# Sparse attention and Fourier mixing on one core: the block sums' share of the values in 64x32 tiles for batches 2 and 3, and batch 0's second weight tile converted behind the copies of the transposed tiles

## The chip, the core and the metric

The kernel runs on one core of one Trainium2 chip. TensorE (PE) multiplies matrices, VectorE (DVE) and ScalarE (ACT) work on elements, GpSimd (POOL) is used a little, and SyncE (SP) issues most DMAs. The metric is the device time of one execution in microseconds (us), as the median of several runs; less is better.

## The reference

The kernel computes attention over a window and over block summaries, then a Fourier mixing with a two-layer network. Cut to what matters:

```python
# q, k, v: (4, 8, 768, 64); block 32, window 16
k_sum = k.reshape(B, H, nb, block, D).max(axis=3)
v_sum = v.reshape(B, H, nb, block, D).mean(axis=3)
scores_l = scale * q @ k.T                      # kept where |i - j| < window
scores_s = scale * q @ k_sum.T + np.log(block)
a = softmax(concatenate([masked scores_l, scores_s]))
x = a @ concatenate([v, v_sum])                 # then (4, 768, 512), heads side by side
mixed = real(fft(fft(x, axis=1), axis=2))
u = x + mixed
un = (u - mean(u)) / sqrt(var(u) + 1e-6)        # over the last axis
out = u + maximum(un @ w_ch1, 0) @ w_ch2        # w_ch1: 512 x 2048, w_ch2: 2048 x 512, float64
```

The two weights come as float64. The kernel converts them to float32 on chip, from their two 32-bit words.

## The kernel before, in words

The four batches run one after another. Each goes through attention (four pairs of heads), the Fourier mixing, a hidden layer and an output layer. TensorE works on one batch's hidden and output layers while the attention of the next batch is fitted in between. Batch 0's attention stands first, in an order written out by hand. After that the order of the instructions on each engine is set at compile time by a planner that takes the ready instruction which the program emits earliest; `high_priority(600)` moves what it wraps ahead, and `issue_after(mark)` puts what it wraps behind the marked instruction of the same engine. DMAs of the first part that go through `fetch` (L549) stay in program order on SP's queue.

**Values of batches 1 to 3** (`values`, L821). One call handles a pair of heads. `av[0]` and `av[1]` are two banks of PSUM. L829 adds the near tokens' share with 48 matmuls: 64 rows of the contraction, 32 output rows, 65 columns; four places of output rows and two halves of the contraction make eight tiles of the array. L834 then adds the block sums' share: for three `t` and two halves `r` one matmul each, with 64 contraction rows, 128 output rows and 130 columns. A reciprocal (L839) and a product (L842) finish the pair's part of `x`. Ahead of it come `scores` (L785), whose exponentials are multiplied by the 0/1 mask `near` (for batch 1's first two pairs not at L802 but at L1051), `sum_scores` (L805), which needs the key maxima `km` (L700), and `scale_sums` (L814).

**Hidden and output layers** (`gen_hidden` L1358, `gen_out` L1414). A product of 2x2 blocks is made with seven products, in three accumulators X, Y and Z. Seven weight blocks per tile are needed: four converted ones and three sums of them (`_left_sums` L477), and seven blocks of the activations `u` (`_right_sums` L483). Hidden tile j starts with the blocks A11 and A12 of its weight tile; only its second use of X and its use of Z need the sums of `u`, and its copies of X and Z are made by ACT (L1388 to L1396), its additions by DVE.

**Weights of batch 0** (`convert` L1099, `make` L1121, `plan` L1072). `words` holds four pieces of raw weight words; a weight tile has two. `exponents` (L1092) takes the exponent bits on DVE (L1096) and rescales them on ACT (L1097); `convert` then takes the mantissa (L1109 on DVE, L1110 on ACT), combines sign and exponent (L1112), adds the low word (L1114) and multiplies (L1116). `make` adds the sums, and stores the tile to DRAM for the later batches. `load_raw` (L1078), called at the start of each conversion, fetches pieces for the tile after it. `plan` lists the tiles in order as (layer, tile, stage): a tile is begun once its stage is in `issued`, and if there is a mark of the stage's name its instructions are put behind that mark.

**Batch 0 between mixing and hidden layer** (`gen_fourier` L1224). After the mixing (L1297, L1299), DVE forms mean and variance and normalises (L1279, mark `mx`), PE transposes the six normalised tiles (L1349), and ACT or DVE copies each to `u` (L1350); the last copy is on DVE and its mark is `u`. Then come the sums of `u`. At L1558 to L1565 `drive` interleaves this with the weights and with the attention of batch 1, which are both written as generators: a step of a generator ends at each `yield`. Of the four attention steps at L1564, the second emits `scores(1, 1)` and `values(1, 0)`, the third `sum_scores(1, 1)` and `load_values(1, 2)`, the fourth the product with `near` for pair (1, 1) and `prepare(1, 2)`, which transposes that pair's queries and keys and takes its key maxima on DVE.

## Time and profile before

| what | us |
|---|---|
| three runs | 792.73, 796.05, 793.62 |
| their median | 793.62 |
| the profiled execution | 790.53 |
| its span, first to last instruction | 788.6 |

The profile shows one execution. PE records are matmuls (PE) and weight loads (PEld); the end of a matmul record is modelled, so the start of the next one is the firmer number. The granted TensorE clock was 0.999 over the span. Groups of the profile that the change touches (count of records, busy time in all, mean of one):

| line, engine, what | records | busy us | mean ns |
|---|---|---|---|
| L829 PE, near share of the values | 1152 | 15.8 | 225 |
| L834 PE, block sums' share of the values | 144 | 12.5 | 291 |
| L1349 PE, transposes of the normalised tiles, batch 0 | 48 | 6.5 | 279 |

Each float32 matmul of the program appears as two records. Of L834's 144 records 96 belong to batches 2 and 3. A timeline line gives start, time, engine, line, operation, out<-in, shapes and count; in brackets stands the idle time before it and what ended it.

### The profile page before, as it was taken

Reading aid. Unit: us, or ns where it says so; the run is one execution under the profiler, and the core shown is the slowest. Engines: PE = TensorE matmul, PEld = TensorE weight load, DVE = VectorE, ACT = ScalarE, POOL = GpSimd, SP = SyncE. Lnnn points to the kernel's source line nnn. Section 1 sums busy time; section 2 is a strip of 40 time slices with the busy share of each in tenths; the row PEclk is TensorE's granted clock in tenths of the full one; section 3 lists DMA queues with packets and bytes.
Section 4 is the critical chain, followed back from the end, with each engine's and each line's share of the span. In section 5 each row is a group of like instructions: output and inputs, shape, how many; then the busy total and the mean of one; then the engine's idle time right before and its main releaser. Section 6 shows DMA issues by size and latency. Waiting matters only on the chain.

```text
span 788.6 us, 14351 instructions
## 1 busy us (share of the span) xinstructions
PE 776.1 (98%) x5920; PEld 562.9 (71%) x5920; DVE 491.2 (62%) x1017; ACT 224.1 (28%) x491; POOL 49.2 (6%) x87
## 2 busy tenths in 40 slices
PE   9999999999999999999999999999999999999997
PEld 6778455445588866787578866788569865886686
DVE  5899978697889566652759545552667623533352
ACT  3565656236536022100236012200136012001200
POOL 0000000000000030200310020300220000000000
PEclk9999999999999999999999999999999999999999
DMA  9999887796855279965442169611513163106001
GB/s 214 184 266 237 206 275 196 242 260 221 232 161 155 49 231 261 204 103 177 154 144 87 54 209 212 184 55 31 223 44 134 54 220 134 47 0 234 0 28 57
DMA packets 133353, 121.82 MB, mean 154 GB/s; under 512 B 94464, under 2 KB 114912, under 8 KB 133088
## 3 DMA queue, kind: packets, MB, share of 16 engines
q1 hardware_dynamic: 132160, 118.53, 53.9%
q0 software_dynamic: 576, 2.10, 0.8%
q8 instruction: 48, 0.79, 0.4%
q10 hardware_dynamic: 544, 0.20, 0.1%
q14 instruction: 25, 0.20, 0.1%
HBM read 97.22 MB, written 23.59 MB: 153 GB/s over the span
## 4 chain that ended last, share of the span: by engine, by line
PE 87%; DVE 9%; ACT 1%; issue 1%; DMA 1%; POOL 0%; SPq 0%; DVEq 0%; POOLq 0%
PE hx L1377 19%; PE ox L1446 18%; PE hz L1377 10%; PE oz L1446 9%; PE hy L1377 5%; PE oy L1446 5%; PE o L1423 4%; PE y L1258 3%; PE sc L793 2%; PE mx L1217 2%; PE av L829 1%; PE av L834 1%; PE qk L718 1%; DVE x L571 1%; PE unt L1349 1%
## 5 line engine op out<-in xcount | busy, mean ns | idle before, releaser
L1377 PE MATMUL hx<-u,w 128*128 128x384 f32 x512 | 185.4, 491 | 1.5 <-ACT h L1394 0.7
L1377 PEld LDWEIGHTS hx<-u,w 128*128 128x128 f32 x512 | 94.9, 190 | 70.3 <-ACT p L800 3.8
L1377 PE MATMUL hz<-u,w 128*128 128x384 f32 x256 | 93.7, 487 | 0.2 <-DVE u L571 0.2
L1446 PE MATMUL oz<-w,s 128*128 128x256 f32 x336 | 81.3, 380 | 0.0
L1446 PE MATMUL ox<-w,s 128*128 128x256 f32 x336 | 80.1, 380 | 0.0
L1446 PE MATMUL ox<-w,h 128*128 128x256 f32 x336 | 79.6, 381 | 0.0
L571 DVE TENSOR_TENSOR x<-ox,x 128x256 f32<-128x256 f32 x84 | 35.5, 423 | 66.2 <-PE ox L1446 65.9
L1377 PEld LDWEIGHTS hz<-u,w 128*128 128x128 f32 x256 | 48.4, 190 | 34.1 <-DVE u L571 0.8
L1446 PEld LDWEIGHTS ox<-w,h 128*128 128x128 f32 x336 | 63.1, 190 | 10.8 <-issue 1.2
L1446 PEld LDWEIGHTS oz<-w,s 128*128 128x128 f32 x336 | 63.3, 190 | 8.9 <-DVE x L571 0.4
L1446 PEld LDWEIGHTS ox<-w,s 128*128 128x128 f32 x336 | 63.2, 190 | 9.0 <-DVE x L571 0.3
L1388 ACT COPY h<-hx 128x384 f32<-128x384 f32 x32 | 15.3, 479 | 187.1 <-PE hx L1377 187.1
L571 DVE TENSOR_TENSOR h<-hy,h 128x384 f32<-128x384 f32 x32 | 17.8, 557 | 48.4 <-PE hy L1377 48.2
L1377 PE MATMUL hy<-u,w 128*128 128x384 f32 x128 | 46.8, 487 | 0.6 <-DVE h L571 0.6
L571 DVE TENSOR_TENSOR h<-hx,h 128x384 f32<-128x384 f32 x32 | 17.8, 556 | 44.1 <-PE hx L1377 43.9
L1423 PE MATMUL o<-w,h 128*128 128x512 f32 x96 | 42.3, 595 | 0.7 <-DVE w L571 0.7
L1407 ACT ACTIVATE h<-hx 128x384 f32<-128x384 f32 x32 | 15.7, 490 | 88.3 <-PE hx L1377 88.2
L1446 PE MATMUL oy<-w,h 128*128 128x256 f32 x168 | 40.1, 380 | 0.0
L571 DVE TENSOR_TENSOR x<-oz,x 128x256 f32<-128x256 f32 x42 | 17.8, 424 | 30.4 <-PE oz L1446 30.1
L1377 PEld LDWEIGHTS hy<-u,w 128*128 128x128 f32 x128 | 24.1, 190 | 16.9 <-DVE h L571 0.7
L1446 PEld LDWEIGHTS oy<-w,h 128*128 128x128 f32 x168 | 31.8, 190 | 4.4
L1423 PEld LDWEIGHTS o<-w,h 128*128 128x128 f32 x96 | 18.0, 190 | 22.7 <-issue 20.7
(167 smaller groups left out, 1072.8 us busy)
## 6 DMA issues: line engine op xcount, KB each, us to landing
w<-dw SPq DMA_DIRECT2D x44, 896.0 KB, 5.7
words<-in_moe_w_ch_dram SPq DMA_DIRECT2D x32, 512.0 KB, 5.7
dw<-w SPq DMA_DIRECT2D x12, 896.0 KB, 7.5
vw<-in_v_dram SPq DMA_DIRECT2D x47, 192.0 KB, 6.1
out_dram<-x SPq DMA_DIRECT2D x23, 256.0 KB, 2.0
vb<-in_v_dram SPq DMA_DIRECT2D x24, 192.0 KB, 6.8
kn<-in_k_dram SPq DMA_DIRECT2D x9, 384.0 KB, 6.1
qn<-in_q_dram SPq DMA_DIRECT2D x9, 384.0 KB, 7.6
```

The lines of the kernel that those rows point to most:

```text
L571: return nc.vector.tensor_tensor(out=out, in0=in0, in1=in1, op=op).ins
L718: nc.tensor.matmul(ps[D * e:D * (e + 1), s:S2:HT], src[:, e, h, s, :], ident, start=True, stop=True)
L793: ins = nc.tensor.matmul(ps[h][r:r + 64, i, :], kt[rows, o:o + 64], qt[rows, o:o + BLOCK], start=True, stop=True)
L829: nc.tensor.matmul(av[r][32 * j:32 * (j + 1), t, :], p[rows, h, i - NB2 * h, :], vw[rows, i, :], start=(t == 0), stop=False, skip_group_ch ...
L834: ins = nc.tensor.matmul(av[r][:, t:t + HT + 1:HT, :], pm[rows, P * t:P * (t + 1)], vs[rows], start=False, stop=(t == HT - 1), skip_group_ ...
L1217: nc.tensor.matmul(out, y[:, g], table, start=False, stop=True, skip_group_check=True)
L1258: nc.tensor.matmul(y, fgs[b][par][:, st, P * g:P * (g + 1)], fs[par][:, g % 2, st, :], start=(st == 0), stop=(st == n - 1))
L1377: ins = nc.tensor.matmul(ps, w[:, a, kk, :], u[:, r, kk, :], start=start and kk == 0, stop=stop and kk == 1, skip_group_check=True)
L1388: nc.scalar.copy(out=c11, in_=X)
L1407: nc.scalar.activation(out=c21, in_=X, func=AF.Relu)
L1423: nc.tensor.matmul(ps, h[:, n, hf, P * t:P * (t + 1)], wt[2, b, j][:, 2 * hf:2 * hf + 2, :], start=(n, hf) == (0, 0), stop=(n, hf) == (NC ...
L1446: nc.tensor.matmul(ps, left[a][:, n, :], wt[2, b, j][:, r, :], start=start and n == 0, stop=stop and n == NC - 1, skip_group_check=True)
```

## The change

In `values` the loop over the output rows is split for batches 2 and 3: instead of one matmul with 128 output rows there are four with 32 rows each, at the four places that L829 uses. Batch 1 keeps 128. In `plan`, weight tile (1, 1) moves from stage `mx` to a new stage `u`, the last copy of the transposed tiles. The product with `near` for pair (1, 1), and those instructions of `prepare(1, 2)` that run on DVE, move behind a new mark `w`, the last of the sums of weight tile (1, 1). The steps at L1564 are emitted in another order: three steps of the attention with the mixing, then fifteen steps of the weights, then the fourth attention step. A helper now remembers the last instruction of `tt`.

```diff
+    final = [None]
+
     def tt(out, in0, in1, op):
-        return nc.vector.tensor_tensor(out=out, in0=in0, in1=in1, op=op).ins
+        final[0] = nc.vector.tensor_tensor(out=out, in0=in0, in1=in1, op=op).ins
+        return final[0]
...
         for t in range(HT):
-            for r in range(2):
-                rows = slice(64 * r, 64 * (r + 1))
-                ins = nc.tensor.matmul(av[r][:, t:t + HT + 1:HT, :], pm[rows, P * t:P * (t + 1)], vs[rows],
-                                       start=False, stop=(t == HT - 1), skip_group_check=True)
+            n = 32 if b > 1 else P
+            for o in range(0, P, n):
+                for r in range(2):
+                    rows = slice(64 * r, 64 * (r + 1))
+                    ins = nc.tensor.matmul(av[r][o:o + n, t:t + HT + 1:HT, :], pm[rows, P * t + o:P * t + o + n], vs[rows],
+                                           start=False, stop=(t == HT - 1), skip_group_check=True)
...
-                    with tc.issue_after(marks["u"]) if g else ExitStack():
+                    with tc.issue_after(marks["w", 1]) if g else ExitStack():
                         (tt if g else gtt)(held[0][:, h], held[0][:, h], near[:, h], ALU.mult)
             if n1 and n1 != (1, 1):
-                prepare(*n1, *((1,) if b > 1 else ()))
+                with tc.issue_after(marks["w", 1]) if n1 == (1, 2) else ExitStack():
+                    prepare(*n1, *((1,) if b > 1 else ()))
...
-    plan = [(1, 0, ("fold", 0)), (1, 1, ("mx", 0)), (1, 2, ("mx", 0)), (2, 0, ("mx", 0)), (1, 3, ("h", 0, 0)), (2, 1, ("mx", 0)),
+    plan = [(1, 0, ("fold", 0)), (1, 1, ("u", 0)), (1, 2, ("mx", 0)), (2, 0, ("mx", 0)), (1, 3, ("h", 0, 0)), (2, 1, ("mx", 0)),
...
             _left_sums(tt, wv)
+            marks["w", j] = final[0]
...
-            if t == NST - 1:
-                marks["u"] = ins.ins
+            if b == 0 and t == NST - 1:
+                marks["u", 0] = ins.ins
+                issued.add(("u", 0))
...
-    drive((mixing, 6, 600), (first(weights, 15), 15, 0), (first(attn, 4), 4, 0))
+    drive((first(attn, 3), 3, 0), (mixing, 6, 600))
+    for _ in first(weights, 15):
+        pass
+    next(attn)
     block_sums(1, 1)
```

## The prediction

> **What bounds the kernel now.** I read the page first: the engine row, then the chain of work that ended last.

> ```profile
> PE 776.1 (98%) x5920; PEld 562.9 (71%) x5920; DVE 491.2 (62%) x1017; ACT 224.1 (28%) x491; POOL 49.2 (6%) x87
> ...
> PE 87%; DVE 9%; ACT 1%; issue 1%; DMA 1%; POOL 0%; SPq 0%; DVEq 0%; POOLq 0%
> ```

> TensorE (PE) is the bound nearly everywhere. The chain's 9% on VectorE (DVE) lies in batch 0 ahead of the first hidden product; for 48 to 105 us DVE is busy almost without a break (windows: 8.00 of 8.00 us in 77 to 85, 7.00 of 7.00 in 90 to 97). So the two parts of the change are priced separately: a PE saving in batches 2 and 3, which reaches the end whole, and a DVE reordering in batch 0.

> Second view, the timeline of PE around one values call of batch 2 (start, time, line, x count of records):

> ```profile
> 309.66 1.20 PE L829 MATMUL av<-vw,p 64*32 64x65 f32 x96
> 310.79 0.94 PE L834 MATMUL av<-vs,p 64*128 64x130 f32 x12
> 311.66 1.24 PE L1377 MATMUL hx<-u,w 128*128 128x384 f32 x3
> ```

> A float32 matmul shows as two records, so L834's 12 are six matmuls. Starts tell more than times: L834's block holds PE for 311.66 - 310.79 = 0.87 us; in the raw starts L829's last record stands 0.145 us before L834's first weight load, and L834's last 0.200 us before the next stage's. All unsplit calls of the two batches show these three numbers.

> Third view, PE's timeline as batch 0 goes from its transposes (unt) to its first hidden products:

> ```profile
> 77.11 1.53 PE L1349 MATMUL unt<-ident,big 128*128 128x128 f32 x12
> 79.46 1.10 PE L811 MATMUL ss<-qt,km 64*32 64x384 f32 x8 [0.82 <-DVE km L700]
> ...
> 85.64 0.91 PE L1377 MATMUL hz<-u,w 128*128 128x384 f32 x2 [0.22 <-DVE u L571]
> 86.94 1.53 PE L1377 MATMUL hx<-u,w 128*128 128x384 f32 x4 [0.38 <-DVE u L571]
> ...
> 95.55 0.91 PE L1377 MATMUL hy<-u,w 128*128 128x384 f32 x2 [0.56 <-DVE h L571]
> ```

> Three things are waited for: the key maxima (km), the sums of u, and a hidden add (h). DVE's timeline says why:

> ```profile
> 77.16 0.69 DVE L1096 TENSOR_SCALAR words<-words 128x1024 int32<-128x1024 int32 x1
> 77.77 0.69 DVE L1109 TENSOR_SCALAR w<-words 128x1024 int32<-128x1024 int32 x1
> 78.37 0.95 DVE L700 TENSOR_REDUCE km<-kt 128x24 f32<-128x768 f32 x1
> 79.23 1.22 DVE L1112 SCALAR_TENSOR_TENSOR words<-words 128x1024 int32<-128x1024 int32 x1
> 80.36 1.23 DVE L1114 SCALAR_TENSOR_TENSOR w<-words,w 128x1024 f32<-128x1024 uint32 x1
> 81.50 1.29 DVE L1350 COPY u<-unt 128x512 f32<-128x512 f32 x2
> 82.70 1.22 DVE L571 TENSOR_TENSOR w<-w,words 128x1024 f32<-128x1024 f32 x1
> 83.83 1.76 DVE L571 TENSOR_TENSOR u<-u 128x1536 f32<-128x1536 f32 x1
> ```

> The conversion of weight tile (1, 1) stands ahead of km, of the copies of the last transposed tiles and of the sums, though hidden tile 0 needs only weight tile (1, 0).

> [...] Here the first 32 records of L829 start 7 ns apart, each group of eight tiles 57 ns after the last. [...] from the 33rd L829 slows to 11.2 ns a record (64 in 716 ns)[...]

> **Part A, the values.** In eight calls (two batches, four pairs) 12 records of L834 become 48, of 32 output rows each, in L829's own mode. Removed: the switch between the two. The cost now, from L829's last start to the next stage's weight load: 0.145 + 0.870 = 1.015 us. After: each of eight tiles gets six records. The moving operand still has 130 columns, and L834's rounds now start 0.112 us apart. First record about 0.06 after L829's last, five steps of 0.112, eight starts of 7 ns (0.05), exit 0.200: 0.87 us, saving 0.145 a call. Bounds: if the first record follows at once (0.017), 0.83 (saving 0.19). [...] If L829's slow pace came from eight moving streams[...], 48 records of twice the columns take 48 x 22.4 ns = 1.08, with 0.200 1.28: a loss of 0.26. Against that last stand the first 32 records, at full pace with the same eight streams. Taken: 8 x 0.145 = **-1.2 us**; ends -1.5 and +2.1. The 288 added record pairs cost nothing[...]; they need one per 0.112/8 = 14 ns. [...]

> **Part B, weight tile (1, 1).** Its instructions on DVE: L1096 0.60, L1109 0.60, L1112 1.13, L1114 1.14, product 1.13, sums 0.33 + 0.60 + 0.33 = 5.9 us; on ACT L1097 1.06 and L1110 0.95. All now follow the copies. PE's excess in the third view, by starts: km 78.37 to 79.46, 1.09 against 0.20 at the earlier unt-to-ss hand-over, 0.89; sums 0.70 and 0.87 against a step of 0.32, 0.38 and 0.55; the add 0.83 against 0.20, 0.63. Together 2.45 us.

> What becomes of each: DVE is free at 77.25, km is done at 78.1, before unt ends: 0.89 gone. The copies run at 78.8 to 79.4, the sums 79.4 to 82.9 instead of 83.8 to 88.2: PE does not wait for them. **Next late is ACT**: the second use of X (hx at 86.94) also needs ACT's copy of X, at 85.72 behind 8.8 us of continuous ACT work from 76.97, which the change shuffles but does not shorten. So hx starts at about 86.2, 0.74 sooner, and with the other half of Z's product (0.65) already done. I take 1.4 us at the end of hidden tile 0, 91.6 instead of 93.0.

> What is added: the near product of pair (1, 1) (two of 0.47) and the key maxima of pair (1, 2) (0.86) wait for tile (1, 1)'s last sum; behind the near product stands values (1, 1), 2.2 us of PE. Tile (1, 1) is ready at 79.4 + 3.5 (sums of u) + 5.9 + 1.2 (x of pair (1, 0)) = 90.0 plus up to 1 us of gaps, just ahead of hidden tile 1's first use at 91.6, so cost nothing; without that cover it is DVE's delay past 91.6. The 0.63 at the hidden add: with DVE's total unchanged I count a third, 0.2. **B = -1.6 us**, ends -3.1 (all 2.45 and the 0.69 that PE waits for a weight tile at 140.37) and +6 (below).

> SP's queue moves too. The loads for the weight tile after (1, 1) stood ahead of the next values' loads:

> ```profile
> 72.81 1.68 SPq L551 DMA_DIRECT2D words<-in_moe_w_ch_dram  x2
> ...
> 81.62 0.81 SPq L551 DMA_DIRECT2D words<-in_moe_w_ch_dram  x2
> ...
> 83.00 6.84 SPq L551 DMA_DIRECT2D vw<-in_v_dram  x4
> ```

> Now the three attention steps are emitted first, so vw's four issues (free to go once values (1, 0) ends, 77) stand ahead: 77 + 6.8 = 84, then the words, landing a median 5.2 us later, 90. DVE wants them at about 91: no cost, with 1 us to spare. POOL's queue has only the near product of pair (1, 0) there (71.31, idle 28 us before), and does not move.

> **Sum.** -1.2 - 1.6 = -2.8 us. The profiled execution took 790.53 us (span 788.6, 1.9 around it), so 787.7 for it; the median shown, 793.62, is 3.1 above it, and carries the same difference: **790.8 us**.

> **Rivals.**
> 1. Whole gain: every excess of B goes, and A is at its best: -3.1 - 1.5 = -4.6, 789.0 us. For it: the delay by the words may let the hidden adds go first on DVE. Against: ACT's 8.8 us.
> 2. B is given back: PE arrives early at 140.37, where it already waits 0.69 us for weight tile (2, 3), whose chain on DVE runs from 111.11 to 140.3 at DVE's own pace. Only A stays: 792.4 us.
> 3. Slower: the words land late. vw's issues at the 8.28 us that an earlier four took and the longest landing of words, 10.4, give 77 + 8.3 + 1.7 + 10.4 = 97.4 instead of 90.14 for the next L1096; in DVE's order the hidden adds and all later weights stand behind it. PE covers some 4 us of that with values and scores, but the weight chain to 140.37 is 7 us late and has 4.0 us idle (105 to 115) less what it needs for loads: I price it at +6. With A's -1.2: 798.4 us. It decides once that L1096 starts after about 94. For it: DMA is at a share of 0.84 to 1.05 there; against: 5.2 is the median landing.
> 4. That part A is no new form: excluded, the output slice alone sets it.

> **Numbers.** Forecast 0.45, rival 1 0.20, rival 2 0.20, rival 3 0.15. About 0.5% (4.0 us) is what a measurement of this kernel can tell from no change. Faster by more: rival 1 and the forecast's upper edge, 0.28; slower by more: most of rival 3, 0.13; within: 0.59. The range leaves out rival 3's far part and spans A's and B's other ends and the runs' own scatter: 787.5 to 796.

> **What would show it.** A: L834's block of 48 records under 0.9 us from L829's last start to the next stage, without a 0.145 hand-over; over 1.0 refutes it. B: km before any L1096 after 77, ss at about 78.6, sums done by 83, hidden tile 1 starting at 91 to 93; the next L1096 before 94, or rival 3 holds. A longer wait than 0.69 for w near 138 is rival 2. A different PE order in batches 2 and 3 would make the sum wrong altogether.

## The result and the profile after

The change makes the kernel slower: 801.24 us (median of six runs, 799.23 to 802.91) against 793.88 (six runs, 791.43 to 796.05), ratio 1.009 with a 95% interval of 1.007 to 1.011. The forecast was 790.8, its range 787.5 to 796.0. The profiled execution took 800.89 us, with a span of 799.1.

The page of the kernel after, the same rows as before (busy time and its share of the span; the chain of work that ended last), and the row of queue q8, whose kind the page calls instruction (packets, MB, share; before the change `q8 instruction: 48, 0.79, 0.4%`):

```profile
PE 776.1 (97%) x6208; PEld 562.1 (70%) x6208; DVE 489.8 (61%) x1017; ACT 224.4 (28%) x491; POOL 49.1 (6%) x87
...
q8 instruction: 51, 0.84, 0.5%
...
PE 85%; DVE 7%; ACT 3%; DMA 2%; issue 2%; SPq 1%; DVEq 0%
```

PE is busy for 776.1 us, exactly as before, with 288 record pairs more. By these sums the loss of 10.5 us in the span is time in which PE stands still; the half clock described below (1.6 us more busy time) and the shorter values calls about cancel in the busy time. In the chain "issue" has risen from 1% to 2%: time in which the engine waited for nothing that the profile shows.

**Where the time is lost.** Each matmul of the one trace is set against its counterpart in the other. The delay of the kernel after, in starts:

| at (us of before) | delay (us) | what happens there |
|---|---|---|
| 77 | +1.1 | batch 0, start of the transposes: late already, 0.6 at 60 |
| 81 | +0.3 | batch 0, end of the transposes |
| 92 | +0.9 | hidden tile 0: waits for ACT |
| 113 | 0.0 | hidden tiles 1 and 2 |
| 122 | +4.4 | hidden tiles 2 and 3: waits for ACT and DVE |
| 145 to 308 | +4.0 to +3.4 | nothing new |
| 323 | +7.9 | batch 2, values of pair 1 |
| 470 | +7.8 | |
| 492 | +10.7 | batch 3, values of pair 0 |
| end | +10.5 | |

Three jumps, then: one of 4.4 us in batch 0, and one each of 4.6 and 2.9 us in two of the eight changed values calls. As this execution was 1.1 us late at 77 us already, batch 0's part of the change costs 4.0 - 1.1 = 2.9 us in it.

**A changed call that goes well.** PE's timeline at batch 2's pair 0:

```profile
295.40 1.14 PE L832 MATMUL av<-vw,p 64*32 64x65 f32 x92
...
296.39 0.91 PE L839 MATMUL av<-vs,p 64*32 64x130 f32 x45
297.24 1.56 PE L1385 MATMUL hx<-u,w 128*128 128x384 f32 x4
```

From the first near matmul to the hidden product after it: 297.24 - 295.40 = 1.84 us, against 311.66 - 309.66 = 2.00 before. The hand-over of 0.145 us is gone; the last records of L832 and the first of L839 even mix, the first of L839 starting 0.06 us ahead of the last of L832.

**The two calls that stop.** The same view at the two jumps:

```profile
314.00 0.78 PE L839 MATMUL av<-vs,p 64*32 64x130 f32 x32
318.16 0.45 PE L839 MATMUL av<-vs,p 64*32 64x130 f32 x13 [3.38 <-issue]
318.53 2.27 PE L1385 MATMUL hx<-u,w 128*128 128x384 f32 x4
...
484.57 0.91 PE L1385 MATMUL hx<-u,w 128*128 128x384 f32 x2
488.41 0.81 PE L1385 MATMUL hx<-u,w 128*128 128x384 f32 x2 [2.92 <-issue]
```

The first stop falls into the middle of one block of matmuls with the same operands: nothing can be waited for there that was not there for the record before. The waits of PE, summed (total, times, longest), put both at the top:

```profile
PE av L839 <- issue: 3.4, 1, 3.4
PE hx L1385 <- issue: 2.9, 1, 2.9
PE hx L1385 <- ACT h L1396: 2.3, 3, 1.7
PE hx L1385 <- DVE h L573: 1.6, 1, 1.6
```

**What stops it.** Number TensorE's recorded instructions (matmuls, weight loads and the few semaphore instructions between them, 12,547 in all) in order of time, from 0. The stops stand ahead of numbers 5825 and 8641, and both leave 193 when divided by 256. From here on a boundary is a place whose number leaves 193, and a block is the 256 instructions behind it. Queue q8 above moves packets of 0.84 MB / 51 = 16 KB. It has 51 of them where TensorE has 12,547 / 256 = 49 blocks, and 48 in the kernel before, where 11,967 recorded instructions make 47. So I take its packets for TensorE's instructions, about one for a block, and call the start of such a packet the fetch of the next block. That is my reading of these counts and of the places of the stops; the experiments test it. At both stops a packet of q8 comes 2.7 and 2.9 us after the previous boundary (at 315.73 and 485.76), takes 1.04 and 1.31 us, and PE goes on 1.4 and 1.3 us after its end. Meanwhile PE had used up its 256 instructions: a changed call is 288 TensorE instructions (matmuls and weight loads of L832 and L839) in 1.8 us, where the old call had 216. In the first stopped call a boundary lies 7 instructions behind the start of the call, so the next one is still inside it; in the second, 37 behind, and the next is 5 instructions behind its end. In the calls that go well and are not cut by other work it lies 76 to 225 behind. Of the 49 boundaries that this trace shows 47 have less than 0.6 us between the starts on their two sides; these two have 3.65 and 3.41 us.

**After the stop.** PE in windows (length; busy PE, PEld, DVE, ACT, POOL; granted clock; DMA share; GB/s):

```profile
313.00:316.00 3.00, 1.78 (x132) 1.51 (x132) 0.34 (x2) 0.85 (x3) 0.00 (x0) 1.00 1.15 350
316.00:318.20 2.20, 0.04 (x7) 0.04 (x8) 0.00 (x0) 0.00 (x0) 0.00 (x0) 1.00 1.00 416
319.30:322.50 3.20, 3.20 (x6) 1.69 (x5) 0.62 (x2) 0.48 (x1) 0.00 (x0) 0.50 1.02 366
323.00:326.00 3.00, 3.00 (x37) 1.66 (x38) 1.14 (x2) 0.79 (x2) 2.84 (x3) 1.00 0.67 97
```

For 3.4 us after the first stop, from 319.24 to 322.65 us, the granted clock is 0.50, and hidden matmuls come 640 ns apart instead of 322: the delay grows from 6.9 to 8.5 us, of which 0.6 is made up again by 323 us. The length of a stop alone does not tell whether the half clock follows: the second stop of this trace (3.4 us from start to start) was not followed by it, while its counterpart in E1 (2.8 us) was. What decides it is not shown.

**Batch 0.** The lines that answer to PE's third view of before:

```profile
78.21 1.53 PE L1356 MATMUL unt<-ident,big 128*128 128x128 f32 x12
79.67 1.17 PE L814 MATMUL ss<-qt,km 64*32 64x384 f32 x8
...
85.34 1.45 PE L1385 MATMUL hz<-u,w 128*128 128x384 f32 x4
88.47 1.56 PE L1385 MATMUL hx<-u,w 128*128 128x384 f32 x4 [1.67 <-ACT h L1396]
...
95.22 1.45 PE L1385 MATMUL hy<-u,w 128*128 128x384 f32 x4
```

The waits for km and for the sums of u are gone; one for ACT of 1.67 us, longer than both together, stands in their place. DVE:

```profile
77.76 0.94 DVE L703 TENSOR_REDUCE km<-kt 128x24 f32<-128x768 f32 x1
...
80.98 0.68 DVE L1102 TENSOR_SCALAR words<-words 128x1024 int32<-128x1024 int32 x1
...
85.85 0.95 DVE L573 TENSOR_TENSOR u<-u 128x768 f32<-128x768 f32 x1
...
92.73 0.42 DVE L573 TENSOR_TENSOR w<-w 128x256 f32<-128x256 f32 x1
93.07 1.02 DVE L573 TENSOR_TENSOR p<-p,near 128x384 f32<-128x384 f32 x2
...
98.75 0.27 DVE L844 RECIPROCAL rec<-av 128x6 f32<-128x6 f32 x2 [1.07 <-PE av L839]
98.99 1.02 DVE L573 TENSOR_TENSOR x<-av,rec 128x384 f32<-128x384 f32 x2
99.92 0.69 DVE L1102 TENSOR_SCALAR words<-words 128x1024 int32<-128x1024 int32 x1
```

The next weight tile's first step (L1102, L1096 before) runs at 99.92 us instead of 90.14. In DVE's order it stands behind the reciprocals of pair (1, 1), which wait for that pair's values on PE (96.60). The product with near, which the change puts behind tile (1, 1)'s last sum (92.73), is done at 94.1, and PE, busy without a break, takes the hy product (95.22) ahead of these values; in the kernel before they started at 93.10, ahead of hy. What comes of it on PE:

```profile
117.30 1.56 PE L1385 MATMUL hz<-u,w 128*128 128x384 f32 x4 [0.90 <-ACT h L1404]
...
119.79 1.56 PE L1385 MATMUL hx<-u,w 128*128 128x384 f32 x4 [0.61 <-DVE w L573]
...
124.19 2.20 PE L1385 MATMUL hx<-u,w 128*128 128x384 f32 x6 [1.55 <-DVE h L573]
```

SP's queue:

```profile
76.86 3.36 SPq L551 DMA_DIRECT2D vw<-in_v_dram  x4
80.32 8.46 SPq L551 DMA_DIRECT2D words<-in_moe_w_ch_dram  x4
```

The first two of these four loads (80.32 and 80.95) bring that weight tile's words. No load of words between 60 and 110 us landed later than 7.5 us after its issue, so they were there by 88.5, 11 us before L1102 reads them.

### The profile page after: what moved, and what is told of

Its sections match the earlier page's. It is cut to its first block, busy times and chain, and to the rows that moved or that the text cites. A ratio compares the mean times of both kernels' runs of the same rounds, so it can differ in the third digit from the quotient of the medians.

```text
span 799.1 us, 14940 instructions
## 1 busy us (share of the span) xinstructions
PE 776.1 (97%) x6208; PEld 562.1 (70%) x6208; DVE 489.8 (61%) x1017; ACT 224.4 (28%) x491; POOL 49.1 (6%) x87
## 4 chain that ended last, share of the span: by engine, by line
PE 85%; DVE 7%; ACT 3%; DMA 2%; issue 2%; SPq 1%; DVEq 0%
PE hx L1385 19%; PE ox L1454 18%; PE hz L1385 9%; PE oz L1454 9%; PE hy L1385 5%; PE oy L1454 5%; PE o L1431 4%; PE y L1265 3%; PE mx L1224 2%; PE sc L796 2%; PE av L832 2%; PE av L839 1%; PE unt L1356 1%; DMA words<-in_v_dram 1%; DMA vb<-in_v_dram 1%
```

## The experiments

Theory: in batches 2 and 3 TensorE stands still until the fetch of its next block is through, so that the loss depends on where a boundary falls, not on the form of the matmuls. Rivals: the form itself; the changed loads of batch 0; more instructions wherever they lie. The numbers of boundaries below come from each kernel's recorded order, as above.

**E1, part A alone**: the `values` part of the diff on the kernel before.

> Part A alone on the kernel before: the block sums' share of batches 2 and 3 in 64x32 tiles, batch 0 as it was. Theory 'instruction blocks': the saving of 0.15 us a call is there (8 x 0.15 = -1.2 us), but TensorE stops twice with nothing waited for, about 3.4 and 2.6 us, 5.2 us after a boundary of 256 instructions that falls into the first 40 instructions of a values call of pair 1 of batch 2 and one of batch 3 (the offsets worked out for this kernel are 11 and 41). Sum: about +4.8 us (ratio 1.006), no delay in batch 0. Rival 'batch 0 costs it all': the stalls come from the changed loads of batch 0 and are gone, -1.2 us (0.9985). Rival 'more instructions, wherever they lie': about +6 us, spread over all eight calls.

Measured: 800.70 us against 793.35, ratio 1.0094 (1.0063 to 1.0124). The stops are where they were worked out to be:

```profile
PE av L836 <- issue: 3.7, 1, 3.7
PE hz L1379 <- issue: 2.3, 1, 2.3
```

Part A alone has the whole loss, and the rival that batch 0's loads cause it is out. The sum was 2.6 us too small: both stops were followed by the half clock (0.50 for 3.4 us), which I had left out.

**E2, part B alone**: the kernel after with `n = P` for all batches.

> Part B alone: the kernel after with the block sums' share in 64x128 tiles again. Theory: batch 0 is 3.3 to 4 us late at 140 us as in the kernel after (the next weight tile's second conversion step on VectorE at about 100 us and not 90), and nothing is lost later: +3 to +3.5 us (ratio 1.004), no idle TensorE over 1 us without a wait in batches 2 and 3. Rival of the prediction (forecast -1.6 us, ratio 0.998) if the delay in the kernel after came through part A. Rival 'two stalls come from part B's loads': +9 us.

Measured: 794.29 against 793.35, ratio 1.0011 (0.9997 to 1.0026): +0.9 us, no "issue" stop over 1 us. In the profile the delay is +1.0 at 77, -0.4 at 113 and +2.7 at 122 us; from 130 us to the end it lies between +1.2 and +2.3. Part B's own loss is smaller than expected; E10 shows why its profile says more than its median.

**E3 and E4, the shift at the start**: 42 small matmuls ahead of everything, with part A and without.

```diff
     weights = gen_weights()
+    ps = abank([1, 1], "pad")
+    for _ in range(42):
+        nc.tensor.matmul(ps, ident[:, 0:1], ident[:, 0:1], start=True, stop=True)
```

> Part A alone, and ahead of everything 42 matmuls of 1x1x1 on the identity (168 TensorE instructions more, their result unused), which shift each later boundary of 256 instructions by 88 to 168 places against the values calls, so that none lies in the first 60 instructions of a call. Theory 'instruction blocks': both stalls are gone, 0.15 us a call saved: -1.2 us and 0 to +1 us for the added matmuls, ratio 0.9985 to 1.000. Rival 'the form of the matmuls stalls by itself, wherever the boundary lies': the same time as part A alone, about +4.8 us, or more.

> The kernel before with the same 42 small matmuls at its start and nothing else: the price of the shift itself. Theory: 0 to +1 us[...]; ratio 1.000 to 1.001. If the shift moves a boundary into a values call of the 216-instruction form and that form stalls too, up to +3 us.

Measured: E3 800.90, ratio 1.0090 (1.0059 to 1.0121); E4 798.44, ratio 1.0066 (1.0047 to 1.0084). Both expectations failed. I had counted the boundaries of pair 1 alone.

```profile
PE av L829 <- issue: 3.2, 1, 3.2
PE av L836 <- issue: 3.1, 1, 3.1
```

These are E3's two longest. In E3 the two old stops are gone, but the shift puts a boundary 4 instructions into batch 2's call of pair 2, and PE stops there for 3.1 us. In both, it also moves one into batch 1's first values call, at 79 us, and PE stops there for 3.1 to 3.2 us, although that call has the old form: with scores and transposes close to it, 256 instructions are used up in 1.84 us of work. The small matmuls themselves take 2.2 us on the path, and at batch 0's start the shift brings two more stops, of 1.8 us in all in E4. So E3's time is the one that the rival "the form of the matmuls" asked for, and the time does not decide; the places do. Both old stops are gone, and a call of the old form stops for 3.1 to 3.2 us.

**E5 and E6, the shift behind batch 0**: 28 or 19 small matmuls in hidden tile 5 of batch 0.

```diff
+            for _ in range(28 if (b, j) == (0, NC + 1) else 0):
+                nc.tensor.matmul(X[0:1, 0:1], w[:, 0, 0, 0:1], u[:, 0, 0, 0:1], start=True, stop=True, skip_group_check=True)
             product(X, A11, B11, True, False)
```

> Part A alone, with 28 matmuls of 1x1x1 (112 TensorE instructions, 28 x 0.053 = 1.5 us) put into batch 0's hidden tile 5, at about 190 us, so behind batch 0's dense stretches and ahead of batch 2's. Worked out from the recorded order of part A alone, this shift leaves no boundary of 256 instructions in the first 60 of the calls at 294, 312, 482 and 504 us; the shortest block with traffic beside it is then one of 3.6 us at 337. Theory 'instruction blocks': no stop in the two calls that stopped, 0 to 1.7 us at 337; -1.2 + 1.5 + 0 to 1.7 = +0.3 to +2.0 us (ratio 1.000 to 1.0025). Rival 'the form itself': both stops stay, about +9 us.

> The same with 19 of the small matmuls (76 instructions, 1.0 us). Worked out in the same way, one boundary falls 3 instructions into batch 2's first values call (at 294 us, its block 1.4 us long), and none into the others. Theory 'instruction blocks': exactly one stop, of 1 to 4 us, in that call, where neither part A alone nor the kernel after has one, and none in the two that stopped: -1.2 + 1.0 + 1 to 4 = +1 to +4 us (ratio 1.001 to 1.005). Rival 'the place in the program': the stops stay in the pair 1 calls.

E6 measured: 796.73 us against 793.47, ratio 1.0041 (1.0022 to 1.0061), +3.3. There is exactly one stop over 0.3 us in batches 2 and 3, in the call that had none in any other kernel so far, where it was worked out to be:

```profile
294.81 0.78 PE L836 MATMUL av<-vs,p 64*32 64x130 f32 x31
298.10 0.68 PE L836 MATMUL av<-vs,p 64*32 64x130 f32 x14 [2.51 <-issue]
```

E5 measured: 800.16, ratio 1.0083 (1.0059 to 1.0107), well over the expected 1.0025. The two stops are gone, but at 337 us the 0 to 1.7 us became 3.44:

```profile
335.12 0.30 PE L793 MATMUL sc<-qt,kt 64*64 64x32 f32 x5
338.87 0.31 PE L793 MATMUL sc<-qt,kt 64*64 64x32 f32 x5 [3.44 <-issue]
```

The block there is used up in 3.6 us, but its fetch starts only 4.2 us after the boundary. From the boundary to the use of the next block it is 7.3 us here, where the stops of the kernel after and of E1 had 5.1 to 5.6. What this depends on is the next question.

**E7, fewer packets beside it**: part A with the loads of later queries and keys in 3 KB rows.

```diff
-    r, o = D * e + 32 * h, (q, k)[n][b, 2 * g + e].offset + 32 * h
-    fetch(out=t[r:r + 32], in_=bass.AP((q, k)[n].tensor, o, [[D, 32], [32 * D, S // 32], [1, 32]]))
+    r, o = D * e + 32 * h, (q, k)[n][b, 2 * g + e].offset + 32 * S * h
+    fetch(out=t[r:r + 32], in_=bass.AP((q, k)[n].tensor, o, [[S, 32], [32, S // 32], [1, 32]]))
```

> Part A alone, with the loads of queries and keys from batch 2, pair 1, on in rows of 3 KB from one place instead of 128 byte pieces: the same bytes in a twenty-fourth of the packets, but the elements in another order, so that these pairs compute on permuted queries and keys. The TensorE stream and its boundaries up to the second stop are those of part A alone. Theory 'the fetch of a block waits behind the kernel's own transfers': in the stopped calls the fetch starts 0.7 to 1.2 us after the boundary (there 2.9 and 2.7), each stop shrinks by about 2 us, to 1.7 and 0.8 us or less: +7.4 - 4 = +3.5 us or less. Rival 'the fetch takes its 5 us whatever else moves': the stops stay at 3.7 and 2.3 us, +7 us.

Measured: 798.66, ratio 1.0064 (1.0039 to 1.0088); the stops are 4.0 and 2.2 us long, as without the edit. But the edit did not do what it was for: in the first stop the transfers still move 415 GB/s (stored weight tiles and values, not queries and keys). It decides nothing on traffic.

**E9, traffic put beside a block that does not stop**, on the kernel before, with TensorE's order unchanged.

```diff
+            if (b, g) == (3, 2):
+                for j in range(8):
+                    fetch(out=junk[j], in_=x[:, :, P:2 * P])
```

> The kernel before, its TensorE order unchanged, with eight stores of finished x of batch 3, pair 1 (393 KB each, to memory that nothing reads) put on the queue behind the last weight loads, from about 507 us on. There the kernel before uses up two blocks of 256 instructions in 3.84 and 3.88 us without a stop, with the transfer engines at a share of 0.01 to 0.3; the fetch of each next block starts 0.74 us after the boundary. Theory 'the fetch of a block waits behind the kernel's own transfers': it starts 1.5 to 3.5 us after the boundary, and TensorE stops 0.3 to 2.5 us with nothing waited for at the end of one or both blocks. Rival 'traffic has no part in it': fetch at 0.7 to 1.0 us, no stop.

Measured (one execution, 793.48 us): of the two blocks there, the first is used up in 3.96 us, its fetch starts 1.3 us after the boundary, and nothing stops. The second needs 3.91 us, its fetch starts 2.8 us after the boundary, and PE stops. A window of each trace inside the second block, first the kernel before, then this one:

```profile
513.00:517.00 4.00, 4.00 (x141) 3.11 (x134) 1.03 (x2) 1.46 (x4) 0.00 (x0) 1.00 0.01 4
```

```profile
516.00:518.00 2.00, 2.00 (x16) 1.25 (x15) 1.03 (x2) 1.34 (x3) 0.00 (x0) 1.00 1.06 299
```

```profile
PE av L831 <- issue: 1.0, 1, 1.0
```

The share of the transfer engines (last but one) goes from 0.01 to 1.06, and with it the start of the fetch from 0.7 to 2.8 us. So, in this one execution, the fetch started later with the added stores beside it. The share is not everything: in the first of the two blocks, with the same share, the fetch came 1.3 us after the boundary, and E3 has a stop of 1.0 us at 531 us with the share at 0.02, after three short blocks in a row (2.4, 3.7 and 3.9 us).

**E10, the kernel before once more**, for a second profile.

> The kernel before, unchanged, for a second profile. In the first, two blocks of batch 0 (from 70.3 and 74.7 us, 4.4 and 5.1 us long) just escape a stop; the executions of part A alone and with the small matmuls, whose batch 0 is the same, stopped there for 1 to 3 us. Theory 'those stops come and go with the execution': TensorE stops 0 to 3 us without a wait between 74 and 83 us, no stop over 0.3 us in the values calls of batches 2 and 3; span 788.5 to 792.5 us.

Measured: 793.47 us, span 791.7, and

```profile
PE sc L793 <- issue: 1.8, 1, 1.8
```

in batch 0 at 76.9 us. The first profile of the kernel before, 790.53 us, had escaped this stop; the other executions with batch 0's old order (E1, E5, E6, E7, E9, E12) stood still there for 1.7 to 4.1 us. Some 2 of the 3 us by which E10's span is longer than the first profile's arise between 66 and 100 us, at this stop and in the half clock behind it. That is most of what the profiled execution lay under the median, and so of the gap between the traces' 10.5 us and the medians' 7.4.

**E8, part B with its loads in the old order**: on E2, so that the words of tile (1, 2) are loaded, and in DVE's order converted, where they were before.

```diff
+    load_raw(6)
     drive((first(attn, 3), 3, 0), (mixing, 6, 600))
```

> Part B alone with the load of weight tile (1, 2)'s words issued ahead of the three attention steps, where it stood before the change. VectorE's order then has that tile's conversion right behind the product of tile (1, 1), and not behind the values of pair (1, 1). Theory 'part B gave its gain back through that order': the second step of tile (1, 2) at 90 to 92 us instead of 99.5, TensorE at 140 us no later than before the change, -0.5 to -1.6 us (ratio 0.998 to 0.9995). Rival 'the wait for tile (1, 1) ahead of the near product is what costs': as part B alone, +0.9 us.

Measured: 794.51 against 793.47, ratio 1.0005 (0.9990 to 1.0020). The step in question (L1102, 99.92 in the kernel after) ran at 95.1 us, in an execution that had lost 3.8 us in batch 0's stops before; less these, 91.3 is the place asked for. The interval takes in both theories, so the order's own price is not settled. What the trace does show is that the new wait for ACT stays whatever the order:

```profile
93.56 1.56 PE L1385 MATMUL hx<-u,w 128*128 128x384 f32 x4 [1.68 <-ACT h L1396]
```

**E11, the kernel after with E6's shift.**

> The kernel after, with the same 19 small matmuls (76 instructions, 1.0 us) in batch 0's hidden tile 5. Worked out from the recorded order: boundaries in the two calls that stopped move to 83 and 113 instructions into them, and one comes 0 to 4 instructions into batch 2's first values call. Theory 'instruction blocks': one stop of 2 to 3 us in that call in place of the two (3.4 and 2.9 us, the first with 1.9 us at half clock behind it): 801.2 + 1.0 - 8 + 2.5 to 4.5 = 796.5 to 798.5 us (ratio 1.003 to 1.006). Rival 'two stops belong to the changed program, wherever boundaries lie': 802 us, 1.010.

Measured: 794.74 us against 793.17, ratio 1.0021 (1.0008 to 1.0034), better than expected: in the profile there is no stop at all, where one was expected. The waits of PE begin with

```profile
PE hx L1385 <- DVE h L573: 2.1, 2, 1.5
PE hx L1385 <- ACT h L1398: 1.7, 1, 1.7
```

Here the boundary falls 1 instruction into batch 2's first call, not 4 as in E6's trace, and the block's fetch starts 2.5 us ahead of it, with the transfers at a share of 0.03. Each against its own runs of the kernel before, the kernel after stands at +7.4 us and E11 at +1.6. So 76 instructions that do nothing take 5.8 us off the kernel after, and with their own 1.0 us the stops were worth 6.8.

**E12, part A alone with the boundaries placed**: 20 small matmuls where PE waits anyway.

```diff
+                    for _ in range(20 if t == 0 and n == NC - 1 else 0):
+                        nc.tensor.matmul(ps[0:1, 0:1], nothing, nothing, start=False, stop=False, skip_group_check=True)
                     for hf in range(2):
                         nc.tensor.matmul(ps, h[:, n, hf, P * t:P * (t + 1)], wt[2, b, j][:, 2 * hf:2 * hf + 2, :],
```

> Part A alone with 20 matmuls of 1x1x1 on zeros (80 instructions, 20 x 0.053 = 1.1 us), added into batch 0's first output tile at about 139 us, just ahead of the 0.7 us that TensorE waits there for a weight tile. Worked out from the recorded order, a boundary of 256 instructions then falls one instruction ahead of batch 2's first values call, whose first matmuls wait for the loaded values, and none in the calls that stopped. Theory: as in the shifted kernel after, the fetch goes before that call starts and nothing stops: -1.2 + 1.1 - 0.7 = -0.8 us (ratio 0.999), the best version these experiments point to. If the fetch there comes late after all, as with 76 instructions, one stop of 2.5 us: +1.7 us (1.002). Rival 'the form itself': +7 us.

Measured: 792.77 us against 793.18, ratio 0.9990 (0.9979 to 1.0002): the size that was expected, but not told from no change. In its profiled execution the two stops of the kernel after were gone, but one that was not expected was left in batch 2's first call: its fetch came 1.2 us after the boundary and not ahead of it.

```profile
PE av L839 <- issue: 1.6, 1, 1.6
```

Blocks of 256 instructions in one table (work: time to use them up, by starts; transfer share: in a window of 1 to 5 us up to or around the start of the fetch; fetch: start of the next block's packet, counted from the boundary that opens this one; stop: the gap in starts at its end):

| kernel, at | work | transfer share | fetch | stop |
|---|---|---|---|---|
| after, 313.0 | 1.5 | 1.15 | +2.7 | 3.6 |
| after, 482.9 | 2.1 | 1.18 | +2.9 | 3.4 |
| E3, 335.8 | 1.5 | 1.20 | +1.8 | 3.3 |
| E6, 293.8 | 1.5 | 0.59 | +1.8 | 2.8 |
| E5, 331.6 | 3.6 | 1.12 | +4.2 | 3.7 |
| E9, 515.2 | 3.9 | 1.06 | +2.8 | 1.3 |
| E9, 511.2 | 4.0 | 1.06 | +1.3 | none |
| E12, 292.9 | 1.6 | 0.21 | +1.2 | 1.9 |
| E3, 526.3 | 3.9 | 0.02 | +2.3 | 1.1 |
| before, 513.5 | 3.9 | 0.01 | +0.7 | none |
| E11, 295.4 | 1.4 | 0.03 | -2.5 | none |
| E7, 360.8 | 1.4 | 0.00 | -1.8 | none |

In every row with a stop PE goes on 1.3 to 1.6 us after the end of the fetch's packet.

## Why the prediction was wrong

**The sum of the parts**: part A's saving -1.2 (from the traces), part B +0.9 (E2), the stops +6.8 (E11): +6.5. Measured: 801.24 - 793.88 = +7.4. The 0.9 between them is within the intervals of E2 and E11; E1 alone would put the stops at 7.35 + 1.2 = 8.6.

**Part A, the saving: right, with some luck.** 0.145 us a call was predicted and 0.16 is there; the hand-over is gone, and it is 0.85 us from L832's last start to the next stage (0.87 was worked out). But two terms are off and cancel: L839's first record starts 0.06 us ahead of L832's last and not 0.06 behind it, and its 48 records take 0.71 us from first start to last, not 0.61. E12's time (-0.4 us by the medians, -0.8 by the ratio) does not contradict -1.2 for the eight calls, but its interval takes in no change.

**Part A, the price of the records: wrong, and this is the step that failed.** The 288 added record pairs were to cost nothing, by an estimate of mine: they need one per 14 ns, and L829's records had come every 11.2 ns. That is the pace inside a call, and it was about right: 48 records in 0.71 us, 15 ns each. Where the stream of instructions comes from was not asked. With 72 instructions more, a call grows from 216 to 288 and is longer than a block of 256. In the two stopped calls a boundary near the start brought the next one after 1.5 and 2.1 us of work, and PE had the next block only 5.1 and 5.6 us after the boundary, with the transfers at a share of 1.15 and 1.18. With 216 instructions even a boundary at the start of a call left 40 instructions of the neighbours in the block; the shortest blocks of the kernel before that begin in the changed calls last 7.6 us at 493 us and 3.8 at 510, the latter with the transfers at 0.19. The range had no case for it: the worst end of part A was +2.1 for eight calls, and the stops cost about 7 in two.

**The half clock** was in no step either. It made the first stop 1.6 us dearer.

**Part B, km: right.** ss follows unt after 79.67 - 78.21 = 1.46 us, 2.35 before: 0.89 gone, as predicted. **The sums: half right.** PE no longer waits for them, but they end at 86.8 us, not 82.9: DVE's order puts one step of the conversion ahead of them and two between them. **Next late is ACT: right in kind, 2.3 us too early.** hx was predicted at 86.2 and starts at 88.47. ACT's copy of X ends at 88.4, behind the copies of the queries, ACT's share of the conversion (85.42) and the block sums; ACT stood idle for 0.93 and 0.97 us around 80, so its 8.8 us moved later instead of staying; 1.1 of the 2.3 us is this execution's lateness at 77. Hidden tile 0 ends at 92.64 + 4 x 0.32 = 93.9 (its last product is the first four of eight records there), against 91.6 predicted and 93.0 before: less the lateness 0.2 gained instead of 1.4. Over the 36 us from the start of the transposes PE stands idle for 1.8 us, 2.2 before: 0.4 us of waiting is gone, not 1.6. The rest of what the table shows as made up by 113 us would lie in PE's changed order; no run took that apart.

**Part B, the added wait: wrong.** Rival 3's point of decision, the next L1096 after 94 us, is passed (99.92), and its consequences are there: the hidden adds and later weights come late, and PE loses 0.90, 0.61 and 1.55 us between 117 and 124. Its reason is not the one I gave: the words did not land late. I priced the wait as DVE's delay alone ("tile (1, 1) is ready ... just ahead of hidden tile 1's first use") and let L1096 follow at about 91; but values (1, 1) now stands behind the hy product in PE's order, its reciprocals stand ahead of L1096 in DVE's order, and DVE waits for PE there (1.07 us). That PE's order changed because near comes later is argued, not tested. Its size, +6, was too large: PE waits 1.9 (E2) and 3.1 us there in the traces, and part B as a whole is at +0.9 (-0.2 to +2.1) in E2's medians. Whether part B also spares the stops of batch 0 stays open: three executions with its order have none, E8 has 3.8 us, and only the first of eight with the old order had none.

**Rivals.** Rival 3 has the right side and part of the mechanism, but the measured 801.24 lies beyond its 798.4 for another reason: batch 0 is the smaller part.

**What stays open**: what sets the start of a fetch besides traffic. E6 and E11 have nearly the same boundary, and one fetch comes 1.8 us after it and the other 2.5 ahead. My guess, which no run shows: a boundary that stands in front of the call's first waits is passed earlier than one behind them. Some of the records fit it: in E6 and E12 the last semaphore instruction ahead of the boundary ends at 293.50 and 292.75, 0.3 and 0.1 us before the boundary, and the fetch is late; in E11 it ends at 291.21, 4.2 us before, and the fetch is early. In the kernel after it ends at 311.12, 1.9 us before, and the fetch is late all the same, with the transfers at 1.15.

## What to carry to other kernels

Before a matmul is cut into smaller tiles, count the instructions of the dense stretch, weight loads too, and ask how long 256 of them last. In the table PE stopped for 1.1 to 3.7 us at the end of blocks that were used up in 1.5 to 3.9 us; other blocks of 1.4 to 4.0 us passed without a stop, and E4 had stops of about 1 us behind blocks of 6.7 and 7.5 us. Eight savings of 0.15 us are 1.2 us, and either of the two stops of the kernel after (3.6 and 3.4 us) took more than that. In that kernel the sign was an "issue" wait of 3.4 us in the middle of equal matmuls. The test was 76 idle instructions far ahead of it, which moved the boundaries: E11 has no stop. All other dense stretches behind such a shift have to be looked at too: in E3 and E5 it brought stops of 3.1 to 3.4 us elsewhere. And where a wait is added, follow the order on the waiting engine through the other engine and back. Here the near product waited for tile (1, 1), the values of its pair came behind the hy product on PE, and on DVE L1102, behind these values' reciprocals, ran at 99.92 us instead of 90.14.
